# K of four chunks first in token halves, loads in that order, Q's first casts on ScalarE, and a general path without SP

## The chip, the core and the metric

The kernel runs on one core of a Trainium2 chip. The metric is the device time of one execution in microseconds. The core has TensorE (PE; its weight loads are shown apart as PEld), VectorE (DVE), ScalarE (ACT), GpSimd (POOL) and SyncE (SP), which issues all loads and stores of the kernel before. TensorE writes its results into eight banks of PSUM, 512 float32 columns of 128 partitions each; VectorE and ScalarE copy them out.

## What is computed

`x` is 2048 tokens by 512, in bfloat16. Two branches read it, and a gate of one number for each token mixes them:

```python
g = _sigmoid((x * gate_w).sum(-1, keepdims=True))
a = _A_ref(x, A_wq, A_wk, A_wv, A_wo, A_beta)
b = _B_ref(x, B_w_gate, B_w_up, B_w_down)
return g * a + (1 - g) * b
```

`_B_ref` is a gated feed-forward: `(gelu(x @ w_gate) * (x @ w_up)) @ w_down`, with 1792 hidden columns. `_A_ref` is attention with 32 heads of 16 columns in four segments of 512 tokens. Each segment has causal softmax attention of its own, and a memory of the segments before it:

```python
logits = jnp.einsum('bhqd,bhkd->bhqk', qs, ks) * scale + mask
p = _softmax(logits, axis=-1)
a_dot = jnp.einsum('bhqk,bhkd->bhqd', p, vs)
pq = phi(qs)
a_mem = num / den          # pq @ M and pq @ z, M and z summed over earlier segments
o = g * a_mem + (1.0 - g) * a_dot
pk = phi(ks)
M = M + jnp.einsum('bhld,bhle->bhde', pk, vs)
```

with `phi(t) = t + 1` for positive `t` and `exp(t)` otherwise, and at the end `o @ wo`.

## The kernel before

**Layout.** Everything is made segment by segment (`NSEG = 4`, 512 tokens). `xS[s % 3]` holds a segment of `x` with columns on partitions, in four blocks (`FC = 4`). K and Q come in four chunks of 128 columns, eight heads each (`NC8 = 4`): `ktb[:, c, :]` and `QT[:, c, :]`, columns on partitions and 512 tokens along the row. For the logits K is stored once more in `KTm`, which has three places (`NK = 3`), with the columns of even or odd heads set to zero (`eo`): two `tensor_scalar` a chunk, on VectorE for the first three chunks of segment 0 and on GpSimd otherwise.

**PSUM.** The pool `pgen` has four one-bank tiles under the tag `gen`, taken in turn by every matrix product. The pool `plg` has one tile of four banks, `lg`, for the logits.

**Start.** `load_inputs` issues loads on SP: `x` of segment 0 in two halves of 256 tokens, then `wk` in two halves of 256 columns (two chunks each), `wq`, the gate vector, `wv`, `beta`, and `wga` in two parts. `x0` is a borrowed buffer, as `x` comes in with tokens on partitions; `warm_up` runs matmuls on constants meanwhile. `transpose_x0` (L175) turns both halves with 16 TensorE transposes, four copies by VectorE and ScalarE putting them into `xS[0]`; the token order inside a half is two rows a partition (`"(p k) d -> p k d"`). Then, in the order of the program text: `u_k` for chunks 0 to 2 (four matmuls of 512 columns, L368; a cast to `ktb`, L305; two `tensor_scalar` to `KTm`, L378), `u_q` for the four chunks (L282, casts by VectorE), `load_rest` (the other segments' `x` by transposing loads, `wup`, `wdn`, `wo`), the gate vector, V (L397, L413), and the 14 gate chunks of segment 0 (L456) with GELU straight from PSUM on ScalarE (L462).

**The visits.** From there a planner orders the work, while the program is built. 72 visits are fixed; each puts up to four banks of logits into `lg` (`group_qk`, L618), ScalarE takes the exponential (L623), GpSimd zeroes the masked corners (L627), and two visits after a chunk's last piece its product with V follows (`pv`, L643). In between, streams of units (K, Q, V, gate G, up U, down D, output O and others) are filled in by a clock of modelled times: TensorE's and ScalarE's time so far and VectorE's backlog. A unit comes when it is allowed and due; `cast` gives a copy out of PSUM to ScalarE where the model shows room there (`near`), else to VectorE. K's chunk 3 of segment 0 is the first unit of stream K. Stores of the output are issued by `u_out` (L515 makes the tile, L519 issues).

**The two paths.** While the visits run, `u_bound` works out a bound on the logits from the largest values of `x`, `wq` and `wk`. At the end of the program text, VectorE compares it with a limit (L1126), every engine, SP too, loads the flag (L1129) and branches (L1130) past `general()`, a second version of the whole computation with the maximum subtracted. With the inputs here `general()` isn't entered. It issues its loads, transposes and stores on SP.

Of the kernel before, what the change touches and what calls it, by code (L numbers as in the profile page):

```python
# [9 lines left out]
dt = mybir.dt  # L10
AF = mybir.ActivationFunctionType
ALU = mybir.AluOpType

P = 128
# [39 lines left out]
def kernel(  # L54
# [29 lines left out]
    def const(shape, dtype, name):  # L84
        return cpool.tile(shape, dtype, name=name, tag=name)
# [37 lines left out]
    safe = const([1, 1], dt.int32, "safe")  # L123

    def gen(name):
        return pgen.tile([P, 512], F32, name=name, tag="gen")

    def x_seg(s):
        nc.sync.dma_start_transpose(xS[s % NX][:, :, :], x2[s * L:(s + 1) * L, :])
# [4 lines left out]
    def load_inputs():  # L134
        half = L // 2
        for i in range(2):
            nc.sync.dma_start(x0[:, 2 * i:2 * i + 2, :],
                              x2[half * i:half * (i + 1), :].rearrange("(p k) d -> p k d", p=P))
        for i in range(2):
            n = slice(D // 2 * i, D // 2 * (i + 1))  # L140
            cols(wk[:, :, n], A_wk[:, n])
        cols(wq, A_wq)
        nc.sync.dma_start(gw4, gate_w.rearrange("(fc p) -> fc p", p=P))
        cols(wv[:, :, 0:D], A_wv)
        nc.sync.dma_start(beta[:, :], A_beta.rearrange("(o n) -> o n", o=1).to_broadcast((P, H)))
        for n in (slice(0, 4 * P), slice(4 * P, DFF)):
            cols(wga[:, :, n], B_w_gate[:, n])
# [27 lines left out]
    def transpose_x0():  # L175
        for half in range(2):
            for f0 in range(0, FC, 2):
                T = pgen.tile([P, 1024], BF, name="x0T", tag="gen")
                for i in range(4):
                    fc, k = f0 + i // 2, i % 2  # L180
                    nc.tensor.transpose(T[:, i * P:(i + 1) * P],
                                        x0[:, 2 * half + k, fc * P:(fc + 1) * P], ident[:, :])
                dst = xS[0][:, f0:f0 + 2, half * 256:half * 256 + 256].rearrange(
                    "q f (p k) -> q f k p", k=2)
                src = T[:, 0:512].rearrange("q (f k p) -> q f k p", f=2, k=2)
                if f0 == 0:
                    nc.vector.tensor_copy(dst, src)
                else:
                    nc.scalar.copy(dst, src)

    def transpose_gw():
        T = pgen.tile([P, 1024], BF, name="gwT", tag="gen")
# [37 lines left out]
    def u_absmax_x(s, periods):  # L230
# [5 lines left out]
                later(periods[fc] - clock[0], g)  # L236
        return 0.0, 0.0, f

    def u_bound():
        def join():  # L240
            nc.vector.tensor_reduce(out=amax[:, 3:4], in_=amax[:, 3:12], axis=mybir.AxisListType.X,
                                    op=ALU.max)
            nc.vector.tensor_tensor(out=amax[:, 0:1], in0=amax[:, 0:1], in1=amax[:, 3:4],
                                    op=ALU.max)
            passed(0.0, 0.4)

        def narrow():
            nc.vector.tensor_copy(amaxb[:, :], amax[:, 0:3])
            passed(0.0, 0.3)

        def spread():
            room_for_bank()
            T = gen("bT")
            for i in range(3):
                nc.tensor.matmul(T[0:1, i * P:(i + 1) * P], lhsT=amaxb[:, i:i + 1],
                                 rhs=ident[:, :], start=True, stop=True)
            nc.vector.tensor_reduce(out=bound[:, 0:3],
                                    in_=T[0:1, 0:3 * P].rearrange("p (i q) -> p i q", i=3),
                                    axis=mybir.AxisListType.X, op=ALU.max)
            passed(0.15, 0.6)  # L260

        def test():
            nc.vector.tensor_tensor(out=bound[:, 3:5], in0=bound[:, 1:3],
                                    in1=bound[:, 0:1].to_broadcast((1, 2)), op=ALU.mult)
            nc.vector.tensor_tensor(out=bound[:, 5:6], in0=bound[:, 3:4], in1=bound[:, 4:5],
                                    op=ALU.mult)
            passed(0.0, 0.4)

        def f():
            later(1, join)  # L270
            later(3, narrow)
            later(5, spread)
            later(7, test)
        return 0.0, 0.0, f
# [15 lines left out]


    limit = [0.0]
    spared = [0.0]

    def near(end):
# [1 line left out]

    def cast(out, src, scale=1.0):
        end = t_pe[0] + MM512
        if near(end):  # L300
            nc.scalar.activation(out, src, AF.Copy, scale=scale)
            t_act[0] = max(t_act[0], end) + CAST_T
            spared[0] = EVAC
        elif isinstance(scale, float):
            nc.vector.tensor_copy(out, src)  # L305
        else:
            nc.vector.tensor_scalar_mul(out, src, scale)
# [51 lines left out]
    def u_phk(s, c):  # L359
        def f():  # L360
            phi(ktb[:, c:c + 2, :], ktb[:, c:c + 2, :], ("k", s, c), 1)
        return 0.0, 0.0, f

    def u_k(s, c):
        def f():
            T = gen("kT")
            for fc in range(FC):
                nc.tensor.matmul(T[:, :], lhsT=wk[:, fc, c * P:(c + 1) * P],  # L368
                                 rhs=xS[s % NX][:, fc, :],
                                 start=(fc == 0), stop=(fc == FC - 1))  # L370
                if fc < FC - 1:
                    yield MM512
            cast(ktb[:, c, :], T[:, :])
            if general_now[0]:
                return MM512
            for p in range(2):
                eng = nc.vector if s == 0 and c < NK else nc.gpsimd
                eng.tensor_scalar(out=KTm[:, (NC8 * s + c) % NK, :, p, :],  # L378
                                  in0=ktb[:, c, :].rearrange("q (b k) -> q b k", b=NB),
                                  scalar1=eo[:, p:p + 1], scalar2=None, op0=ALU.mult)  # L380
            return MM512
        return 4 * MM512, EVAC, f

    pk_at = {}

    def u_pk(s, c):
        def f():
            assert ("k", s, c - c % 2) in ready
            nc.sync.dma_start_transpose(pk[:, :, c * P:(c + 1) * P], ktb[:, c, :])
            pk_at[s] = clock[0]  # L390
        return 0.0, 0.0, f

# [52 lines left out]
    def u_vs(s):  # L445
        def f():
            v, w = V[s % 2], Vs[s % 2]
            nc.sync.dma_start(w[0:64, :, 0:VE], v[64:128, :, 0:VE])
            nc.sync.dma_start(w[64:128, :, 0:VE], v[0:64, :, VE:2 * VE])
        return 0.0, 0.0, f  # L450

    def u_gate(s, hs, direct):
# [52 lines left out]
    def u_out(s, qt):  # L505
        def f():
            T = gen("aT")
            oT = oTs[s]
            for fc in range(FC):
                nc.tensor.matmul(T[:, :], lhsT=oT[:, fc, qt * P:(qt + 1) * P], rhs=wo[:, fc, :],  # L510
                                 start=(fc == 0), stop=(fc == FC - 1))
                if fc < FC - 1:
                    yield MM512
            osb = tBs[(s, qt)][:, :]
            nc.vector.scalar_tensor_tensor(out=osb, in0=T[:, :],  # L515
                                           scalar=gct[:, s, qt:qt + 1],
                                           in1=osb, op0=ALU.mult, op1=ALU.add)
            q0 = s * L + qt * P
            nc.sync.dma_start(out2[q0:q0 + P, :], osb)  # L519
            return MM512  # L520
        return 4 * MM512, EVAC, f

# [73 lines left out]
    def mem_num(s, c):  # L596
        assert general_now[0] or (count(("Mn", s)) > c // 2 and count(("inv", s)) > c // 2)
        T = gen("mn")
        for qq in range(KT):
# [8 lines left out]
        nc.sync.dma_start_transpose(mT[:, :].rearrange("p (q t) -> p q t", q=KT),  # L608
                                    tm[:, :, :, :].rearrange("p q h d -> p (q h d)"))
        tms[(s, c)] = mT  # L610

    def group_qk(pieces):
# [55 lines left out]
    load_inputs()  # L668
    make_identity(nc, ident[:, :])
    warm_up()  # L670
    transpose_x0()
    setup_consts()


# [91 lines left out]
            for _ in u[2]():  # L766
                pass

    for c in range(NK):
        run(u_k(0, c))  # L770
    for c in range(NC8):
        run(u_q(0, c))
    load_rest()
    transpose_gw()
    for kt in range(KT):
# [289 lines left out]

    def general():
        general_now[0] = True
        nc.gpsimd.memset(Macc[:, :, :, :], 0.0)
        nc.vector.tensor_copy(hm[:, :], bm[:, :, 16])
        for s in range(NSEG):  # L1070
            oT = wk2.tile([P, FC, L], BF, name="oT", tag="oT")
            oTs[s] = oT
            if s % NX == 0:
                x_seg(s)
            for c in range(NC8):
                run(u_k(s, c))
                run(u_q(s, c))
# [40 lines left out]
            if s < NSEG - 1:  # L1118
# [4 lines left out]
                for half in range(2):  # L1123
                    run(u_M(s, half))

    nc.vector.tensor_scalar(out=safe[:, :], in0=bound[:, 5:6],  # L1126
                            scalar1=float(DH ** 0.5 * D * D), scalar2=EXP_LIMIT,
                            op0=ALU.mult, op1=ALU.is_le)
# [31 lines left out]
```

## Time and profile before

| what | value |
|---|---|
| median of 3 runs | 270.8 us (270.6 to 270.86) |
| the profiled execution | 270.57 us |
| its span in the profile | 268.8 us |
| busy: TensorE, VectorE, ScalarE, GpSimd | 262.3, 203.7, 209.0, 156.8 us |
| granted clock of TensorE, mean over the span | 0.996 |
| first K matmul, first Q matmul, first gate matmul | 5.83, 8.50, 15.69 us |
| last output tile made, last store issued | 265.38, 265.41 us |
| DMA | 16.6 MB, mean 62 GB/s over the span |

The span runs from the first instruction that the profiler saw to the last one; the execution's own time is 1.7 us longer. Busy time of TensorE counts a matmul until its modelled end, so that one of 512 columns shows 0.38 us although the next starts 0.216 us after it. In a profile line `L368 PE MATMUL kT<-x,wk` is: line of the kernel, engine, operation, what it writes and reads. `<-` behind an idle time names what ended it.

### The profile page before, as it was taken

What the parts mean: (1) busy time and instruction counts of PE and PEld (TensorE: products, weight loads), DVE (VectorE), ACT (ScalarE), POOL (GpSimd) and SP (SyncE); (2) the same over time, 40 slices, a digit from 0 to 9 for tenths busy, and PEclk for the clock granted to TensorE, in tenths of its full rate; (3) what the DMA queues carried; (4) which work ended last, traced back from release to release, by engine and by line L of the source; (5) the groups of instructions that cost most, each with busy time, mean ns of one, the idle gap of its engine ahead of it and who ended that gap; (6) DMA issues with size and microseconds to landing.
All of it is one profiled execution on the core that took longest, in us unless ns stands there. A gap on an engine that the chain in (4) does not pass through costs nothing.

```text
span 268.8 us, 6576 instructions
## 1 busy us (share of the span) xinstructions
PE 262.3 (98%) x2713; PEld 117.5 (44%) x2713; DVE 203.7 (76%) x390; ACT 209.0 (78%) x163; POOL 156.8 (58%) x298
## 2 busy tenths in 40 slices
PE   7999999999999999999999999999999999999993
PEld 3454434344453444445444444444444544344441
DVE  2999575868777887697986979596898588697374
ACT  3237889999997998889999988889888987567420
POOL 4000168897905979987811998596875089654400
PEclk9999999999999999999999999999999999999998
DMA  6999901200160000301052002110000200001102
GB/s 205 334 211 321 331 18 35 41 4 0 29 136 2 0 22 22 78 4 41 0 68 56 2 21 50 33 34 8 20 24 21 66 2 20 19 3 41 39 22 85
DMA packets 30282, 16.60 MB, mean 62 GB/s; under 512 B 20008, under 2 KB 28968, under 8 KB 30248
## 3 DMA queue, kind: packets, MB, share of 16 engines
q1 hardware_dynamic: 30248, 16.14, 22.9%
q8 instruction: 22, 0.36, 0.6%
q14 instruction: 12, 0.10, 0.1%
HBM read 8.14 MB, written 2.10 MB: 38 GB/s over the span
## 4 chain that ended last, share of the span: by engine, by line
PE 86%; POOL 5%; issue 4%; DMA 2%; ACT 1%; SPq 0%; DVE 0%; ACTq 0%; DVEq 0%; POOLq 0%
PE gT L456 19%; PE uT L477 17%; PE dT L493 14%; PE lg L618 8%; PE od L643 6%; PE aT L510 5%; PE qT L282 5%; PE kT L368 5%; PE vT L397 4%; POOL pT L627 3%; POOL KTm L378 2%; DMA wk<-in_A_wk_dram 2%; PE MT L531 1%; PE mn L600 1%; ACT pT L623 1%
## 5 line engine op out<-in xcount | busy, mean ns | idle before, releaser
L627 POOL TENSOR_SCALAR_AFFINE_SELECT pT<-pT 64x256 bf16<-64x256 bf16 x256 | 113.8, 445 | 94.2 <-ACT pT L623 81.4
L623 ACT ACTIVATE pT<-lg 128x2048 bf16<-128x2048 f32 x72 | 135.1, 1876 | 24.9 <-PE lg L618 21.6
L477 PE MATMUL uT<-x,wup 128*128 128x512 bf16 x224 | 60.4, 380 | 0.0
L456 PE MATMUL gT<-x,wga 128*128 128x512 bf16 x224 | 57.0, 380 | 0.0
L493 PE MATMUL dT<-wdn,G 128*128 128x512 bf16 x224 | 52.9, 380 | 0.0
L483 DVE TENSOR_TENSOR G<-uT,G 128x512 bf16<-128x512 f32 x56 | 38.1, 684 | 6.4 <-PE uT L477 6.2
L378 POOL TENSOR_SCALAR KTm<-ktb,eo 128x512 bf16<-128x512 bf16 x26 | 40.6, 1572 | 1.3
L650 DVE STREAM_TRANSPOSE oq<-od 128x512 f32<-128x512 f32 x32 | 21.0, 695 | 19.5 <-PE od L643 19.5
L493 PEld LDWEIGHTS <-G 128*128 128x128 bf16 x224 | 20.8, 98 | 25.0 <-issue 2.1
L456 PEld LDWEIGHTS <-wga 128*128 128x128 bf16 x224 | 20.5, 98 | 23.9 <-issue 2.2
L477 PEld LDWEIGHTS <-wup 128*128 128x128 bf16 x224 | 19.8, 97 | 24.0 <-issue 5.4
L618 PE MATMUL lg<-QT,KTm 32*128 32x192 bf16 (+7 forms) x512 | 28.5, 287 | 0.0
L305 DVE CAST G<-gT 128x512 bf16<-128x512 f32 x24 | 16.5, 688 | 9.7 <-PE gT L456 9.5
L618 PEld LDWEIGHTS <-KTm 32*128 32x128 bf16 x512 | 8.3, 92 | 28.4 <-issue 28.1
L643 PE MATMUL od<-pT,V 64*32 64x128 bf16 (+7 forms) x512 | 19.4, 284 | 0.2 <-POOL pT L627 0.2
L643 PE MATMUL od<-pT,Vs 64*32 64x128 bf16 (+7 forms) x512 | 19.4, 284 | 0.0
L471 ACT ACTIVATE G<-G 128x3584 bf16<-128x3584 bf16 x6 | 18.8, 3182 | 0.0
L656 DVE SCALAR_TENSOR_TENSOR o<-oq,ogs,rden 128x256 bf16<-128x256 f32 x32 | 17.0, 532 | 1.1
L368 PE MATMUL kT<-x,wk 128*128 128x512 bf16 x64 | 16.8, 380 | 0.9 <-DMA wk<-in_A_wk_dram 0.9
L282 PE MATMUL qT<-x,wq 128*128 128x512 bf16 x64 | 16.6, 379 | 0.0
L515 DVE SCALAR_TENSOR_TENSOR tB<-aT,gct,tB 128x512 bf16<-128x512 f32 x16 | 11.9, 746 | 6.0 <-PE aT L510 5.7
L510 PE MATMUL aT<-wo,oT 128*128 128x512 bf16 x64 | 16.5, 380 | 0.0
(96 smaller groups left out, 274.8 us busy)
## 6 DMA issues: line engine op xcount, KB each, us to landing
out_dram<-tB SPq DMA_DIRECT2D x16, 128.0 KB, 1.7
wup<-in_B_w_up_dram SPq DMA_DIRECT2D x1, 1792.0 KB, 8.4
wdn<-in_B_w_down_dram SPq DMA_DIRECT2D x1, 1792.0 KB
wga<-in_B_w_gate_dram SPq DMA_DIRECT2D x1, 1280.0 KB, 10.2
Vs<-V SPq DMA_DIRECT2D x8, 144.0 KB, 2.6
G<-in_A_x_dram SPq DMA_DIRECT2D x2, 256.0 KB, 2.8
wk<-in_A_wk_dram SPq DMA_DIRECT2D x2, 256.0 KB, 4.2
wq<-in_A_wq_dram SPq DMA_DIRECT2D x1, 512.0 KB, 5.7
```

The lines of the kernel that those rows point to most:

```text
L282: nc.tensor.matmul(T[:, :], lhsT=wq[:, fc, c * P:(c + 1) * P], rhs=xS[s % NX][:, fc, :], start=(fc == 0), stop=(fc == FC - 1))
L368: nc.tensor.matmul(T[:, :], lhsT=wk[:, fc, c * P:(c + 1) * P], rhs=xS[s % NX][:, fc, :], start=(fc == 0), stop=(fc == FC - 1))
L378: eng.tensor_scalar(out=KTm[:, (NC8 * s + c) % NK, :, p, :], in0=ktb[:, c, :].rearrange("q (b k) -> q b k", b=NB), scalar1=eo[:, p:p + 1], ...
L456: nc.tensor.matmul(T[:, :], lhsT=wga[:, fc, hs * P:(hs + 1) * P], rhs=xS[s % NX][:, fc, :], start=(fc == 0), stop=(fc == FC - 1))
L477: nc.tensor.matmul(T[:, :], lhsT=wup[:, fc, hs * P:(hs + 1) * P], rhs=xS[s % NX][:, fc, :], start=(fc == 0), stop=(fc == FC - 1))
L483: nc.vector.tensor_tensor(out=g, in0=T[:, :], in1=g, op=ALU.mult)
L493: nc.tensor.matmul(T[:, :], lhsT=G[s % NG][:, hs, qt * P:(qt + 1) * P], rhs=wdn[:, hs, :], start=(hs == 0), stop=(hs == HS - 1))
L510: nc.tensor.matmul(T[:, :], lhsT=oT[:, fc, qt * P:(qt + 1) * P], rhs=wo[:, fc, :], start=(fc == 0), stop=(fc == FC - 1))
L618: nc.tensor.matmul(lg[:, j, off:off + n], lhsT=KTm[rows, i % NK, b].rearrange("r p k -> r (p k)"), rhs=QT[rows, i % NC8, 64 * b:L], start= ...
L623: nc.scalar.activation(pT[:, :, :], lg[:, :, :], AF.Exp, scale=DH ** -0.5)
L627: nc.gpsimd.affine_select(out=v, in_=v, pattern=[[0, 4], [1, 64]], compare_op=ALU.is_ge, fill=0.0, base=0, channel_multiplier=-1)
L643: nc.tensor.matmul(od[p][32 * j:32 * j + 32, 64 * b:L], lhsT=w[:, 18 * h:18 * h + 32], rhs=t[rows, j, off:off + n], start=(b == 0), stop=( ...
```

## The change

1. `load_inputs` issues `x` half, `wk` half, `x` half, `wk` half, and `wq` in two halves of 256 columns; `x`'s halves are laid out with whole blocks of 128 tokens, `"(k p) d -> p k d"`, so that the copies after the transposes write contiguous tokens.
2. `first_k` replaces `transpose_x0` and the three `u_k`. It takes one four-bank tile of the pool of `lg`, a bank for each chunk. In order: transposes of the first `x` half; the first token half of chunks 0 and 1; transposes of the second half; the first token half of chunks 2 and 3; then the second token half of each chunk, and behind each its copy, on VectorE with the two `KTm` steps for chunks 0 to 2, on ScalarE for chunk 3.
3. Chunk 3's unit in stream K is now `u_km`, only its two `KTm` steps on GpSimd, when a place in `KTm` is free.
4. While the first four `u_q` are issued, `on_act` sends their casts to ScalarE.
5. The flag is computed twice: `is_safe(0)` right after the bound, which GpSimd loads, and `is_safe(1)` at the end for TensorE, VectorE and ScalarE. SP doesn't load the flag. `general()` issues its loads and stores on GpSimd and transposes by TensorE (`turn`).

```diff
     def load_inputs():
...
         for i in range(2):
             nc.sync.dma_start(x0[:, 2 * i:2 * i + 2, :],
-                              x2[half * i:half * (i + 1), :].rearrange("(p k) d -> p k d", p=P))
-        for i in range(2):
+                              x2[half * i:half * (i + 1), :].rearrange("(k p) d -> p k d", p=P))
             n = slice(D // 2 * i, D // 2 * (i + 1))
             cols(wk[:, :, n], A_wk[:, n])
-        cols(wq, A_wq)
+        for n in (slice(0, D // 2), slice(D // 2, D)):
+            cols(wq[:, :, n], A_wq[:, n])
...
+    def is_safe(i):
+        nc.vector.tensor_scalar(out=safe[:, i:i + 1], in0=bound[:, 5:6],
+                                scalar1=float(DH ** 0.5 * D * D), scalar2=EXP_LIMIT,
+                                op0=ALU.mult, op1=ALU.is_le)
...
-            passed(0.0, 0.4)
+            is_safe(0)
+            passed(0.0, 0.5)
...
     def cast(out, src, scale=1.0):
         end = t_pe[0] + MM512
-        if near(end):
+        if on_act[0]:
+            nc.scalar.copy(out, src)
+        elif near(end):
...
+    def first_k():
+        T = plg.tile([P, 4, 512], F32, name="lg", tag="lg")
+
+        def part(c, half):
+            t = slice(256 * half, 256 * half + 256)
+            for fc in range(FC):
+                nc.tensor.matmul(T[:, c, t], lhsT=wk[:, fc, c * P:(c + 1) * P], rhs=xS[0][:, fc, t],
+                                 start=(fc == 0), stop=(fc == FC - 1))
+
+        transpose_x0(0)
+        part(0, 0)
+        part(1, 0)
+        transpose_x0(1)
+        part(2, 0)
+        part(3, 0)
+        for c in range(NC8):
+            part(c, 1)
+            if c < NK:
+                nc.vector.tensor_copy(ktb[:, c, :], T[:, c, :])
+                k_masked(0, c)
+            else:
+                nc.scalar.copy(ktb[:, c, :], T[:, c, :])
...
-            nc.sync.dma_start(out2[q0:q0 + P, :], osb)
+            queue[0].dma_start(out2[q0:q0 + P, :], osb)
...
-    for c in range(NK):
-        run(u_k(0, c))
+    first_k()
     for c in range(NC8):
+        on_act[0] = True
         run(u_q(0, c))
+    on_act[0] = False
...
-        us.append(unit(u_k(s, c), first(i) - 12, ("k", s),
+        us.append(unit((u_km if i < NC8 else u_k)(s, c), first(i) - 12, ("k", s),
...
     def general():
         general_now[0] = True
+        queue[0] = nc.gpsimd
...
-    nc.vector.tensor_scalar(out=safe[:, :], in0=bound[:, 5:6],
-                            scalar1=float(DH ** 0.5 * D * D), scalar2=EXP_LIMIT,
-                            op0=ALU.mult, op1=ALU.is_le)
-    ok = nc.values_load(safe[0:1, 0:1])
+    flag = nc.alloc_registers("safe", engines=[mybir.EngineType.PE, mybir.EngineType.DVE,
+                                               mybir.EngineType.Activation,
+                                               mybir.EngineType.Pool])
+    is_safe(1)
+    for reg in flag:
+        i = 0 if reg.engine == mybir.EngineType.Pool else 1
+        nc.reg_load(reg, safe[0:1, i:i + 1])
+    ok = nc.snap(flag, min_val=0, max_val=1)
     with tc.If(ok == 0, preferred_fallthrough_block=True, label="safe"):
         general()
```

In the built program TensorE's matmuls of the main path are 2713 before and 2729 after.

More of the change, by code (lines that the diff above doesn't have):

```diff
@@ L122 @@
     bound = const([1, 8], F32, "bound")
-    safe = const([1, 1], dt.int32, "safe")
+    safe = const([1, 2], dt.int32, "safe")
     def gen(name):
         return pgen.tile([P, 512], F32, name=name, tag="gen")
+    queue = [nc.sync]
     def x_seg(s):
@@ L173, in warm_up, with transpose_x0 @@
                              start=True, stop=True, tile_position=(64 * r, 32 * j))
[L175 to L189, printed above, removed]
+    def transpose_x0(half):
+        for f0 in range(0, FC, 2):
+            T = pgen.tile([P, 1024], BF, name="x0T", tag="gen")
+            for i in range(4):
+                fc, k = f0 + i // 2, i % 2
+                nc.tensor.transpose(T[:, i * P:(i + 1) * P],
+                                    x0[:, 2 * half + k, fc * P:(fc + 1) * P], ident[:, :])
+            dst = xS[0][:, f0:f0 + 2, half * 256:half * 256 + 256]
+            src = T[:, 0:512].rearrange("q (f t) -> q f t", f=2)
+            if f0 == 0:
+                nc.vector.tensor_copy(dst, src)
+            else:
+                nc.scalar.copy(dst, src)
     def transpose_gw():
@@ L292 @@
     limit = [0.0]
+    on_act = [False]
     spared = [0.0]
@@ L362, in u_phk, with k_masked @@
         return 0.0, 0.0, f
+    def k_masked(s, c):
+        for p in range(2):
+            eng = nc.vector if s == 0 and c < NK else nc.gpsimd
+            eng.tensor_scalar(out=KTm[:, (NC8 * s + c) % NK, :, p, :],
+                              in0=ktb[:, c, :].rearrange("q (b k) -> q b k", b=NB),
+                              scalar1=eo[:, p:p + 1], scalar2=None, op0=ALU.mult)
     def u_k(s, c):
@@ L367, in f @@
             for fc in range(FC):
-                nc.tensor.matmul(T[:, :], lhsT=wk[:, fc, c * P:(c + 1) * P],
-                                 rhs=xS[s % NX][:, fc, :],
+                nc.tensor.matmul(T[:, :], lhsT=wk[:, fc, c * P:(c + 1) * P], rhs=xS[s % NX][:, fc, :],
                                  start=(fc == 0), stop=(fc == FC - 1))
@@ L373, in f, with u_km, turn @@
             cast(ktb[:, c, :], T[:, :])
[L374 to L380, printed above, removed]
+            if not general_now[0]:
+                k_masked(s, c)
             return MM512
         return 4 * MM512, EVAC, f
+    def u_km(s, c):
+        def f():
+            k_masked(s, c)
+        return 0.0, 0.0, f
+    def first_k():
[16 more added lines that the diff above has]
+                k_masked(0, c)
+            else:
+                nc.scalar.copy(ktb[:, c, :], T[:, c, :])
+    def turn(dst, src):
+        T = pgen.tile([P, 1024], BF, name="tT", tag="gen")
+        for i in range(KT):
+            nc.tensor.transpose(T[:, i * P:(i + 1) * P], src[:, i, :], ident[:, :])
+        nc.vector.tensor_copy(dst, T[:, 0:512].rearrange("p (i t) -> p i t", i=KT))
     pk_at = {}
@@ L388, in f @@
             assert ("k", s, c - c % 2) in ready
-            nc.sync.dma_start_transpose(pk[:, :, c * P:(c + 1) * P], ktb[:, c, :])
+            if general_now[0]:
+                turn(pk[:, :, c * P:(c + 1) * P], ktb[:, c, :].rearrange("p (k t) -> p k t", k=KT))
+            else:
+                nc.sync.dma_start_transpose(pk[:, :, c * P:(c + 1) * P], ktb[:, c, :])
             pk_at[s] = clock[0]
@@ L447, in f @@
             v, w = V[s % 2], Vs[s % 2]
-            nc.sync.dma_start(w[0:64, :, 0:VE], v[64:128, :, 0:VE])
-            nc.sync.dma_start(w[64:128, :, 0:VE], v[0:64, :, VE:2 * VE])
+            queue[0].dma_start(w[0:64, :, 0:VE], v[64:128, :, 0:VE])
+            queue[0].dma_start(w[64:128, :, 0:VE], v[0:64, :, VE:2 * VE])
         return 0.0, 0.0, f
@@ L607, in mem_num @@
         mT = wk2.tile([P, L], BF, name="mT", tag="mT")
-        nc.sync.dma_start_transpose(mT[:, :].rearrange("p (q t) -> p q t", q=KT),
-                                    tm[:, :, :, :].rearrange("p q h d -> p (q h d)"))
+        mTv = mT[:, :].rearrange("p (q t) -> p q t", q=KT)
+        if general_now[0]:
+            turn(mTv, tm[:, :, :, :].rearrange("p q h d -> p q (h d)"))
+        else:
+            nc.sync.dma_start_transpose(mTv, tm[:, :, :, :].rearrange("p q h d -> p (q h d)"))
         tms[(s, c)] = mT
@@ L670 @@
     warm_up()
-    transpose_x0()
     setup_consts()
@@ L1073, in general @@
             if s % NX == 0:
-                x_seg(s)
+                rows = G[(s + 1) % NG][:, 0:KT, :]
+                nc.gpsimd.dma_start(rows, x2[s * L:(s + 1) * L, :]
+                                    .rearrange("(k p) d -> p k d", p=P))
+                for fc in range(FC):
+                    turn(xS[s % NX][:, fc, :].rearrange("p (k t) -> p k t", k=KT),
+                         rows[:, :, fc * P:(fc + 1) * P])
             for c in range(NC8):
```

## The prediction

> **What bounds the kernel now.** I read the page's busy shares first, then a table of stretches, then TensorE's waits, then the chain of the first 30 us, and last VectorE's timeline of the start and the program's end. The page's first line of shares:
>
> ```profile
> PE 262.3 (98%) x2713; PEld 117.5 (44%) x2713; DVE 203.7 (76%) x390; ACT 209.0 (78%) x163; POOL 156.8 (58%) x298
> ```
>
> The table of stretches: start and end, length, then busy time and instructions of PE, PEld, DVE, ACT and POOL, granted clock, DMA share, GB/s:
>
> ```profile
> 28.00:120.00 92.00, 92.00 (x998) 40.54 (x995) 70.70 (x134) 82.60 (x62) 66.69 (x120) 1.00 0.20 49
> 120.00:200.00 80.00, 79.98 (x920) 36.30 (x919) 64.31 (x124) 72.34 (x56) 56.45 (x103) 1.00 0.14 30
> 200.00:250.00 50.00, 49.72 (x517) 22.05 (x516) 38.40 (x80) 38.91 (x25) 28.64 (x56) 1.00 0.09 23
> ```
>
> From 28 to 250 us TensorE is hardly ever out of work, while ScalarE and VectorE have 10 to 23% of slack. So whatever delays TensorE's stream before 28 us delays the end by as much, and matmuls taken out of the later stream are saved. TensorE's waits for others (us in total, times, longest), but for one of 1.0 before the warm-up:
>
> ```profile
> PE kT L368 <- DMA wk<-in_A_wk_dram: 0.9, 1, 0.9
> PE od L643 <- POOL pT L627: 0.2, 1, 0.2
> ```
>
> The chain of waits at the start (start, us, what):
>
> ```profile
> 1.71 4.07 DMA wk<-in_A_wk_dram
> 5.78 0.05 issue
> 5.83 2.76 PE kT L368 x12
> 8.59 3.54 PE qT L282 x16
> ```
>
> TensorE waits once, for the first half of `wk`, then runs on without a break: K of three chunks, Q, V. One landing at 5.78 sets when everything starts. VectorE meanwhile (start, duration, instruction):
>
> ```profile
> 6.90 0.69 DVE L305 CAST ktb<-kT 128x512 bf16<-128x512 f32 x1 [1.18 <-PE kT L368]
> 7.63 0.62 DVE L378 TENSOR_SCALAR KTm<-ktb,eo 128x512 bf16<-128x512 bf16 x2
> 8.16 0.69 DVE L305 CAST ktb<-kT 128x512 bf16<-128x512 f32 x1
> 8.88 0.61 DVE L378 TENSOR_SCALAR KTm<-ktb,eo 128x512 bf16<-128x512 bf16 x2
> 9.41 0.68 DVE L305 CAST ktb<-kT 128x512 bf16<-128x512 f32 x1
> ```
>
> It takes 1.26 us a chunk against TensorE's 0.86 (4 matmuls of 0.216), and this costs nothing: each chunk has a bank of its own from a pool of four, so TensorE is at Q's matmuls while VectorE still drains K.
>
> The span is 268.8 us, this execution 270.57, so 1.7 us lie around the span; the median of the runs is 270.8, that is 0.23 above it.
>
> **The start, to the second x half.** The loads go x half, `wk` half, x half, `wk` half. Before, they land at 3.50, 4.17 (x) and 5.78, 6.55 (`wk`), and `wq` at 8.46. After, the first megabyte is the same four pieces, x in rows of 1 KB instead of 2 KB (packets of 46 ns against 84, so about 0.1 us more a half). I expect 3.6, 4.7 to 5.2, 5.3 to 6.0 and 6.7. TensorE's eight transposes of the first half run at 3.85 (0.056 us each); the copies behind them end 1.25 (VectorE) and 1.47 us (ScalarE) after the transposes' start, as in the first half of before (5.02 and 5.24 less 3.77): 5.1 and 5.3. Chunks 0 and 1, first token half: 8 matmuls of 256 columns at half of 0.216, 0.86 us, 5.15 to 6.0. Second transposes to 6.5. Chunks 2 and 3 need the second `wk` half: 6.75 to 7.6. The second half's copies end near 7.5, beside them. So the second token half begins at t0 = 7.6 (7.3 if the contiguous copies are quicker than the 0.72 us of the strided ones and `wk` lands early; 8.3 if pieces land 0.7 us late, as `wk`'s first half did when 1.61 us passed between it and the x half before it).
>
> **The second token half is the large term.** All four chunks now lie in one four-bank tile `T` of the pool `lg`. In the built program's list of instructions and waits, the first matmul of chunk 1's second half waits for VectorE's copy of chunk 0, chunk 2's for the copy of chunk 1, chunk 3's for that of chunk 2: the tile is guarded as a whole, though each chunk has its own bank. Behind the waiting matmul stand, in TensorE's order, the other chunks, then Q, V and everything else. One round: three matmuls until the last one starts 0.32, its completion 0.27 (0.379 for 512 columns at a pitch of 0.216 leaves 0.16 of latency, plus 0.107), handover 0.04 (6.87 to 6.90), copy 0.69, handover 0.05 (5.78 to 5.83): 1.37 us. VectorE's own round of 1.26 fits inside it. Without the wait it would be 0.43. Three rounds and a last 0.43: Q's matmuls begin at 7.6 + 3 x 1.37 + 0.43 = 12.15 instead of 8.50: **+3.65 us**. A round lies between 1.26 (VectorE alone) and 1.45.
>
> The Trainium skill, "PSUM — Partial Sum Buffer" (Terms, PSUM bank), keeps engines apart per bank and quadrant alone; by it these waits aren't needed and the start would come out as in the first rival. The trace agrees on the rule (chunk 1's matmuls at 6.70 run while VectorE casts chunk 0 at 6.90), but the wait is in the program.
>
> **Chunk 3 of K** leaves the later stream, where TensorE has no gap to hide it: 4 x 0.216 = **-0.86 us**. If TensorE then merely idles there, 0. `k_masked` stays on GpSimd for it (2 x 1.57 us, idle 42% of the span), due at the same visit.
>
> **Q's casts on ScalarE.** Four of about 0.69 us (L301's length) and chunk 3's copy go there, 3.4 us. ScalarE takes chunk 3 at 12.4, Q from 13.2 to about 16.5, then `eb` 0.23 and a table load of 1.28, done at 18.0; its first GELU is wanted at about 20.3. V's first bank must be free at 15.7 and is at 14.8; the last V bank is wanted at 18.0, free at 16.5. So nothing; without that cover up to 0.7. VectorE loses 2.48 us of casts, where it limits nothing.
>
> **The loads behind.** One more issue on SP's queue (0.5 us) and `wq` in 512-byte pieces move `wv` from 9.84 to about 10.4 and the first `wga` part from 12.5 to 13.2; they are wanted at 15.8 and 19.3. The transposing loads of x behind them wait for a VectorE memset that now comes at about 12.3 (13.1 before). Nothing.
>
> **The program's end.** The last rows are
>
> ```profile
> 264.63 0.75 DVE L515 SCALAR_TENSOR_TENSOR tB<-aT,gct,tB 128x512 bf16<-128x512 f32 x1
> 265.29 0.13 DVE L1126 TENSOR_SCALAR safe<-bound 1x1 int32<-1x1 f32 x1
> 265.41 0.33 SPq L519 DMA_DIRECT2D out_dram<-tB  x1
> ```
>
> The last store lands 1.67 us after its issue, at 267.08. SP loads the flag and branches until 266.46, and from 266.93 goes through eight semaphore waits of L1130 and eight of L1155, 0.06 to 0.09 us each, to 268.09; a closing barrier follows. After, SP has no flag and no L1130; it has four waits for GpSimd's DMA counts, which pass at once, and eight for its own. The last of 65 loads and stores counts on the first of these eight, so seven remain after its landing: 7 x 0.063 and two drains of 0.07, 267.68: **-0.4 us** (0 to -0.6). GpSimd's early flag, load and branch (0.49 + 0.05 us) and its setting of those counts come after its last select at 253.1, with 12 us of cover; with the late flag SP's four waits would stand behind it, 0.5 us at most. The general path is not entered; its longer lists cost nothing that a row shows.
>
> **The order of the work between.** The planner's visits are shuffled from about visit 5 to the last fifth (the last 64 groups of TensorE are alike). The old order loses 0.3 us or more in one go at three places only, 1.1 us in all, so I take 0, between -0.6 and +0.6.
>
> **Sum.** 3.65 - 0.86 - 0.4 = +2.4 us: 272.95 for a profiled execution like this one, 273.2 on the median.
>
> **Rivals.** (1) *The waits cost nothing*, because VectorE is done in time or the order holds without them: Q begins at 7.6 + 4 x 0.43 = 9.33, +0.83; less 0.86 and 0.4 that is -0.4; ScalarE's Q casts then queue behind VectorE's three rounds (chunk 3's copy waits for chunk 2's) and V's first bank comes up to 0.4 late: 270.4 to 270.8, not slower, below 270.2 only with t0 at 7.3. It decides if a round takes under 0.6 us. Against it: the cast alone takes 0.69. Chance 0.08.
> (2) *The clock falls.* Three idle stretches of 0.94 us between 8 and 12 us: if TensorE then ran at the 0.43 us a matmul of the warm-up rows (2.31 us for 5) for 2.2 us or until Q's end, 1.1 to 3.5 us more: about 275.5. Against it: 1.08 us of idling at 4.75 was followed by matmuls at 0.216, granted clock 1.00. Chance 0.04. The Trainium skill, "TensorE: Matmul & The Clock Gate" (A second HAM failure mode), tells of such falls from short idling between groups of matmuls; the trace's one gap didn't show it.
> (3) *Chunk 3's time isn't got back*, because ScalarE's exponentials pace the visits: 273.2 + 0.86 = 274.1. For it: ScalarE is 90% busy from 28 to 200. Against: TensorE is 100% busy there. Chance 0.10.
>
> **How the numbers follow.** The forecast's case has 0.72, these three 0.22, and 0.06 is for what I don't see (a planner order that wins or loses over 0.6 us). Its own bounds, taken together as squares: down 0.3 (t0), 0.33 (rounds), 0.2 (end), 0.6 (order): 0.8; up 0.7, 0.24, 0.4, 0.6: 1.0. With rival 3 inside, the range is 272.2 to 274.4. A measurement of this kernel can tell about 0.2% (0.54 us) from no change: faster by more 0.04 (half of rival 1, and a lucky order), within 0.06, slower 0.90.
>
> **What would show it.** In the profile after: TensorE idle 0.9 us before three of the K matmuls, each ended by VectorE's copy of `ktb`; VectorE's copies about 1.37 apart; Q's first matmul near 12.15; the first gate matmul near 19.3 (15.69); from the last store's issue to the span's end 3.0 us instead of 3.4. Wrong if K's matmuls of the second half follow each other without waits, if Q's matmuls take 0.43 us, or if the stretch from the first gate matmul to the last output matmul isn't 0.9 us shorter.

## The result, and the profile after

The changed kernel takes 275.04 us (median of six executions, 274.40 to 276.25) against 270.77 us for the kernel before in the same job (six executions, 270.51 to 270.90): a ratio of 1.0153, 95% interval 1.0127 to 1.018. It is slower, as forecast, but by 4.3 us where the sum had 2.4, and 275.04 lies 0.64 us above the range. The profiled execution took 274.40, the shortest of the six. That matters below: a second profile shows where a usual one loses more.

The page's first line of shares:

```profile
PE 263.6 (97%) x2729; PEld 119.4 (44%) x2729; DVE 201.3 (74%) x387; ACT 210.5 (77%) x167; POOL 156.6 (57%) x298
```

TensorE is as dominant as before. The same table of stretches (start and end, length, busy time and instructions of PE, PEld, DVE, ACT and POOL, granted clock, DMA share, GB/s):

```profile
28.00:120.00 92.00, 92.00 (x980) 40.33 (x979) 69.04 (x128) 81.78 (x65) 62.54 (x111) 1.00 0.20 46
120.00:200.00 80.00, 79.49 (x924) 36.52 (x923) 64.75 (x123) 71.34 (x54) 56.99 (x104) 1.00 0.13 30
200.00:250.00 50.00, 49.21 (x516) 21.86 (x514) 39.81 (x84) 38.61 (x26) 28.93 (x57) 1.00 0.09 23
```

The second and third stretch have lost 0.5 us of TensorE's time each: 79.98 and 49.72 became 79.49 and 49.21. Small as that looks, it is where the largest miss of the forecast lies. TensorE's waits (us in total, times, longest) name both losses; the wait for the engine's own start and one of 0.3 are left out:

```profile
PE lg L405 <- DVE ktb L417: 2.3, 3, 0.8
PE uT L524 <- ACT V L310: 1.0, 2, 0.5
...
PE od L693 <- POOL pT L677: 0.2, 1, 0.2
PE lg L405 <- DMA wk<-in_A_wk_dram: 0.2, 1, 0.2
```

The first line is the wait that the prediction described. The second was not in it. A wait counts here from the modelled end of the last matmul, so the stream loses more than the line says: 0.95 us three times in the first, 0.68 us twice in the second, counted from where the next matmul could have started.

The chain of waits at the start (start, us, what):

```profile
2.34 4.54 DMA wk<-in_A_wk_dram
6.88 0.05 issue
6.93 1.50 PE lg L405 x12
8.43 0.02 issue
8.45 0.70 DVE ktb L417
9.15 0.04 issue
9.20 0.61 PE lg L405 x4
9.81 0.02 issue
9.83 0.70 DVE ktb L417
```

Matmuls and copies take turns: four matmuls, VectorE's copy, four matmuls. The copies start at 8.45, 9.83 and 11.21, so a round is 1.38 us (forecast 1.37), and Q's first matmul is at 12.39 (forecast 12.15, before 8.50).

What the two waits of the second kind are, in the timeline of ScalarE and then of TensorE around 131 us (start, duration, instruction, idle time before):

```profile
129.78 1.88 ACT L673 ACTIVATE pT<-lg 128x2048 bf16<-128x2048 f32 x1 [0.25 <-PE lg L668]
131.56 0.54 ACT L310 ACTIVATE V<-vT 128x448 bf16<-128x448 f32 x1
```

```profile
130.77 0.36 PE L444 MATMUL vT<-wv,x 128*128 128x448 bf16 x1
130.97 0.67 PE L578 MATMUL MT<-V,pk 128*128 128x136 bf16 x8
132.15 0.38 PE L524 MATMUL uT<-x,wup 128*128 128x512 bf16 x1 [0.51 <-ACT V L310]
```

V's matmuls end at 131.1. The planner has given their cast to ScalarE, which is in an exponential from 129.78, so the cast starts only at 131.56 and ends at 132.10. Of the four banks of `pgen`, the next one `uT` needs is the one this cast empties, and TensorE stands still from the end of MT's matmuls to 132.15. The same happens at 200.0 to 200.74. In the order of before, no `uT` matmul waits for a cast of V.

The program's end:

```profile
268.87 0.75 DVE L562 SCALAR_TENSOR_TENSOR tB<-aT,gct,tB 128x512 bf16<-128x512 f32 x1
269.54 0.13 DVE L240 TENSOR_SCALAR safe<-bound 1x1 int32<-1x1 f32 x1
```

The last store is issued at 269.65 and the span ends 3.02 us later, instead of 3.43.

So the span splits in three: the start, the work from the first gate matmul to the last store, and the end. The experiments are in the same table.

| us | first K, first Q matmul | first gate matmul | last store issued | gate to last store | last store to span end | median |
|---|---|---|---|---|---|---|
| before | 5.83, 8.50 | 15.69 | 265.41 | 249.72 | 3.43 | 270.77 to 270.84 |
| changed | 4.89, 12.39 | 19.57 | 269.65 | 250.09 | 3.02 | 275.04 |
| changed, second profile (f6) | 4.89, 12.96 | 20.13 | 270.25 | 250.12 | 3.02 | 274.99 |
| e1: copies last | 4.89, 10.07 | 17.25 | 267.33 | 250.08 | 3.02 | 272.21 |
| e2: order of before | 4.89, 13.03 | 20.20 | 269.70 | 249.51 | 3.02 | 274.45 |
| e3: e1 and e2 | 4.89, 10.14 | 17.31 | 267.18 | 249.87 | 3.02 | 271.72 |
| e4: flag alone | 6.07, 8.67 | 15.85 | 265.56 | 249.71 | 2.60 | 269.99 |
| f1: e1, two casts out | 4.89, 10.08 | 17.25 | 266.51 | 249.26 | 3.02 | 271.31 |
| f4: e4, `wq` in halves | 5.94, 8.54 | 15.72 | 265.43 | 249.71 | 3.02 | 270.40 |

### The profile page after: what moved, and what is told of

It reads as the page before. It is cut to its first block, busy times and chain, and to the rows that moved or that the text cites. A ratio compares the mean times of both kernels' runs of the same rounds, so it can differ in the third digit from the quotient of the medians.

```text
span 272.7 us, 6617 instructions
## 1 busy us (share of the span) xinstructions
PE 263.6 (97%) x2729; PEld 119.4 (44%) x2729; DVE 201.3 (74%) x387; ACT 210.5 (77%) x167; POOL 156.6 (57%) x298
## 4 chain that ended last, share of the span: by engine, by line
PE 84%; POOL 5%; issue 4%; ACT 2%; DMA 2%; DVE 1%; SPq 1%; ACTq 0%; DVEq 0%; POOLq 0%
PE gT L503 18%; PE uT L524 17%; PE dT L540 14%; PE lg L668 8%; PE od L693 5%; PE aT L557 5%; PE qT L288 5%; PE vT L444 4%; PE kT L384 3%; POOL pT L677 3%; POOL KTm L376 2%; ACT pT L673 2%; DMA wk<-in_A_wk_dram 2%; PE lg L405 1%; PE MT L578 1%
## 5 line engine op out<-in xcount | busy, mean ns | idle before, releaser
L314 DVE CAST G<-gT 128x512 bf16<-128x512 f32 x27 | 18.5, 685 | 5.9 <-PE gT L503 5.7
L693 PEld LDWEIGHTS <-V 64*32 64x32 bf16 x512 | 13.1, 92 | 5.9 <-issue 3.5
```

The source lines that it names most:

```text
L693: nc.tensor.matmul(od[p][32 * j:32 * j + 32, 64 * b:L], lhsT=w[:, 18 * h:18 * h + 32], rhs=t[rows, j, off:off + n], start=(b == 0), stop=( ...
```

## The experiments

The theory after the first profile: (A) the start loses what the shared tile's waits cost, (B) the gain of chunk 3 is eaten by the two V casts that the reshuffled order puts behind an exponential, (C) the end gains what SP no longer does. The rival to B is that TensorE was held up by ScalarE in any order, so that chunk 3's time could never be got back.

**e1, the copies after all matmuls (A).**

```diff
         for c in range(NC8):
             part(c, 1)
+        for c in (3, 0, 1, 2):
             if c < NK:
```

> The changed kernel, but first_k issues the second token halves of all four chunks before any copy, then the copies (ScalarE's chunk 3 first, then VectorE's three). TensorE's matmuls then wait for no copy. Theory A (the three waits on the shared tile cost about 2.85 us): Q's first matmul moves from 12.39 to about 9.6 us and the median from 275.0 to about 272.2. Rival B (the time is lost behind the start): median stays within 0.5 us of 275.0. If the idle stretches at the start also cause the spread of the runs (274.4 to 276.25) by lowering TensorE's clock in some executions, the spread shrinks to some 0.4 us and the mean clock is 1.00 in all runs.

Measured: 272.21 us (five executions, 271.89 to 272.26), ratio 1.0045 (1.0032 to 1.0058). TensorE's timeline:

```profile
4.89 1.68 PE L405 MATMUL lg<-x,wk 128*128 128x256 bf16 x8
6.56 0.62 PE L182 MATMUL x0T<-ident,G 128*128 128x128 bf16 x8
7.44 2.79 PE L405 MATMUL lg<-x,wk 128*128 128x256 bf16 x24 [0.26 <-DMA wk<-in_A_wk_dram]
```

The 24 later matmuls follow each other with no wait, and Q starts at 10.07. The expected 9.6 was taken from the changed kernel's first profile; here the second half of `wk` lands at 7.40 instead of 6.88. The median of 272.2 was met, as the usual execution of the changed kernel loses that time too (f6 below). The same copies are made on the same engines, three of them at the same 0.69 us, and 2.8 us of the 4.3 are gone. A is shown: the waits, not the amount of work, cost this. The executions lie within 0.37 us of each other, as the text expected if the gaps also caused the spread of the changed kernel's; its other sign, a mean clock of 1.00 in all of them, did not come (two have 0.997; in the profiled one of these the only half clock recorded comes at the end, from 268.91 us on).

**e2, the order of before (B); e3, both.** The planner is told that `u_km` still takes four matmuls and a cast, and the bound as long as before; nothing of chunk 3's matmuls or cast is issued. All work behind the start then comes in the order of before, with a hole at chunk 3's old place. (Theory C of the two texts that follow is B here.)

```diff
             is_safe(0)
-            passed(0.0, 0.5)
+            passed(0.0, 0.4)
...
     def u_km(s, c):
         def f():
+            for fc in range(FC - 1):
+                yield MM512
+            end = t_pe[0] + MM512
+            if near(end):
+                t_act[0] = max(t_act[0], end) + CAST_T
+                spared[0] = EVAC
             k_masked(s, c)
-        return 0.0, 0.0, f
+            return MM512
+        return 4 * MM512, EVAC, f
```

> The changed kernel, but the planner is told that chunk 3 of K still takes four matmuls and a cast at its old place (nothing is computed there), so that all later work stands in exactly the order of before. Theory C (the shuffled order costs TensorE two stalls of 0.68 us behind V's casts on ScalarE): the stalls are gone, the stretch from the first gate matmul to the last output tile is 0.86 us shorter than before's, and the median is about 273.7. Rival D (order is noise, the rest comes from elsewhere): 275.0.

> Both edits of the two runs before. If A and C add up: 275.0 - 2.85 - 1.3, about 270.9. If the old order gives TensorE nothing once its start is early (it waits for ScalarE's exponentials instead): about 272.

Measured: e2 274.45 us (four executions, 273.92 to 274.48), ratio 1.0126 (1.0111 to 1.0141); e3 271.72 (seven, 271.43 to 272.05), ratio 1.003 (1.0019 to 1.0041). Gate to last store is 249.51 and 249.87 in place of 250.09: the two V waits are gone, but most of the 0.86 isn't back. e3's 0.36 over e2 is one more wait for GpSimd, at 230.6 us. e2's timeline of ScalarE and of TensorE shows why:

```profile
44.88 1.88 ACT L680 ACTIVATE pT<-lg 128x2048 bf16<-128x2048 f32 x1 [0.17 <-PE lg L675]
```

```profile
45.63 0.59 PE L510 MATMUL gT<-x,wga 128*128 128x512 bf16 x2
46.81 0.40 PE L675 MATMUL lg<-QT,KTm 32*128 32x512 bf16 x4 [0.58 <-ACT pT L680]
```

The next logits need the banks of `lg`, and the exponential holds them until 46.76. Chunk 3's four matmuls had filled that time, as the chain of the kernel before shows at the same place:

```profile
40.31 0.97 PE kT L368 x4
41.28 0.86 PE qT L282 x4
42.15 0.43 PE gT L456 x2
```

Without them TensorE stands 0.74 us. So in the old order the rival holds: there ScalarE's exponential sets the pace at that place.

**f1, e1 without the two casts (B, directly).** V's chunk 2 in segments 2 and 3 isn't cast, so those rows keep what an earlier segment left; the time is what is read here.

```diff
         elif near(end):
-            nc.scalar.activation(out, src, AF.Copy, scale=scale)
+            if not skip:                     # u_v: skip=(s, kt) in ((2, 2), (3, 2))
+                nc.scalar.activation(out, src, AF.Copy, scale=scale)
```

> The changed kernel with its copies in an order of their own (as e1_copies_last), and two of V's casts left out: chunk 2 of segments 2 and 3, the two that ScalarE made behind an exponential while TensorE stood at uT (0.68 us each, at 129.1 and 197.7 us of e1_copies_last). The rows of V that they would write keep what an earlier segment left there. Everything else stays in its place. Theory (the two stalls are what ate the gain of the removed K chunk): no gap between MT and uT at those two places, first gate matmul to last store 248.7 instead of 250.08, median 272.21 - 1.36 = 270.85. Rival (TensorE would meet another wait at once, the casts only showed it): 0.5 us or less comes back, 271.7 or more, and gate to last store stays above 249.5.

Measured: 271.31 us (twelve executions, 270.64 to 271.56), ratio 1.0 (0.9979 to 1.0022); gate to last store 249.26. That lies between the two expectations: 0.82 of the 1.36 us came back. Neither place shows a wait any more, but a new one is there 5 us behind the first. VectorE, then TensorE:

```profile
134.44 0.68 DVE L533 TENSOR_TENSOR G<-uT,G 128x512 bf16<-128x512 f32 x1
```

```profile
135.17 0.59 PE L527 MATMUL uT<-x,wup 128*128 128x512 bf16 x2 [0.44 <-DVE G L533]
```

VectorE empties an older `uT` at 134.44 to 135.12, as in e1 (134.41), where TensorE came 0.7 us later and found the bank free. Of the first place's 0.68 us, 0.60 is paid again to VectorE; the second place's 0.68 is a true gain. Without this wait gate to last store would be 248.66 by these rows, 1.06 under before; no run shows that. So B is right about what held TensorE, and the rival about half of what a removed wait is worth.

**e4, the flag and SP's part alone on the kernel before (C); f4, the same with `wq` in two loads.** e4 is the kernel before with part 5 of the change. f4 adds

```diff
-        cols(wq, A_wq)
+        for n in (slice(0, D // 2), slice(D // 2, D)):
+            cols(wq[:, :, n], A_wq[:, n])
```

> The kernel before with only the last part of the change: SP out of the general path, early flag for GpSimd, general path with GpSimd's loads and TensorE's transposes; same order of work as before. Theory E: from the last store's issue to the span's end 3.0 instead of 3.4 us, median 270.4. Rival F (the closing barrier ends with another engine, or GpSimd's part of the path costs as much): 270.8.

> The kernel before with the SP-free general path and early flag alone (as e4_flag_only), and wq's load in two halves: 65 loads and stores by SP in place of 64. Theory (the program's end reads one semaphore after another, and the last store's place among the eight decides how many are read after it): last store to span end 3.0 instead of 2.60, median 269.99 + 0.42 = 270.4, the rest unchanged. Rival (the end is shorter for another reason in e4_flag_only, the load order or the start): 2.6 again, 270.0.

Measured: e4 269.99 us (twelve executions, 269.74 to 272.15) against 270.83 in its job, ratio 0.9979 (0.9958 to 1.0001), last store to span end 2.60. f4 270.40 (twelve, 270.11 to 270.67), ratio 0.9971 (0.9951 to 0.9992), end 3.02. The trace of SP's closing reads explains the 0.42. In e4 the last of 64 loads and stores is counted on the last of eight semaphores; by its landing at 267.23 the other seven have been read (266.18 to 267.01), and the eighth at 267.25 is the last. In f4 the last of 65 is counted on the first; SP waits there until the landing at 267.09 and then reads seven more, 0.06 us each, to 267.53. C is shown. The 3.0 and 270.4 expected for e4 were missed: they held the reads that follow in a kernel with 65 loads and stores, and e4 has 64. The interval of e4's ratio just reaches 1, f4's doesn't. The end is two terms: -0.83 for SP out of the last path, +0.42 for one load more.

**f6, the changed kernel again.**

> The changed kernel once more, unaltered, for a second profile, because its first profiled execution (274.40) was the shortest of six with a median of 275.04. Theory (in a usual execution the second half of x lands later, as in e1, e2 and e3, at 6.5 to 6.6 where the first profile had 6.10): begin of the second token half at about 8.3, Q's first matmul at 12.8 to 13.1, span 273.1 to 273.4, and gate to last store 250.0 to 250.2 as before. Rival (the start is the same and the rest varies): Q at 12.4, and gate to last store 250.5 or more.

Measured: the profiled execution 275.13, span 273.28, Q at 12.96, gate to last store 250.12; all as expected. The chain's two lines that differ:

```profile
2.34 5.11 DMA wk<-in_A_wk_dram
...
7.50 1.50 PE lg L405 x12
```

`wk`'s second half lands at 7.45 instead of 6.88, and `x`'s second half at 6.56 instead of 6.10. All of the 0.6 us between the two spans is there. e1, e2, e3 and f1 had 6.46 to 6.64 too, so the first profile is the exception, and the later start is the usual one.

**f2, g1, g2, g3: why the loads land late.** Before, the third load landed at 5.78. Is it the pieces of 1 KB, or the order? f2 and g2 are e1 with `x` in pieces of 2 KB, `"(p k) d -> p k d"`, and the strided copies of before; g3 is e1 with both `x` halves ahead of both `wk` halves; g1 is e1 again.

```diff
# g3
             nc.sync.dma_start(x0[:, 2 * i:2 * i + 2, :], ...)
+        for i in range(2):
             n = slice(D // 2 * i, D // 2 * (i + 1))
```

> The changed kernel with its copies in an order of their own (as e1_copies_last), and x loaded in rows of two tokens (2 KB pieces) as in the kernel before, so that the copies of the transposes are strided again; the order of the loads stays the new one. Theory (the pieces of 1 KB make x's second half land late, 6.5 us in e1, e2 and e3 against 5.8 to 6.0 for the third load of the old order): x's second half lands at 5.8 to 6.0, Q's first matmul at 9.7 to 9.9 (0.5 earlier landing, 0.3 back in the strided copy), median 272.0. Rival (the size of the pieces does nothing; the third load is late for another reason): it lands at 6.3 to 6.6 again, Q at 10.1 to 10.4, median 272.2 to 272.5.

> e1_copies_last once more, unaltered, on the same chip as the two that follow, since f2 (median 272.57) and e1 (272.21) were timed in different jobs. Both theories: x's second half lands at 6.4 to 6.6, Q's first matmul at 10.0 to 10.3, median 272.2 to 272.4.

> f2_2kb_rows once more (e1 with x in pieces of 2 KB, the copies strided). Theory (1 KB pieces delay x's second half): it lands at 5.9 to 6.1 again, Q at 9.7 to 9.9, and the median is 0.2 to 0.4 under g1's. Rival (one profile's chance): it lands at 6.3 to 6.6, and the median is g1's or up to 0.3 above it, because of the strided copies.

> e1 (x in pieces of 1 KB) with the loads in the order of the kernel before: both halves of x, then both halves of wk. Theory (what the start pays beside the waits is the order: x's second half comes third instead of second, and 16 first-half and second-half groups can't run until it is there): x's second half lands at 4.2 to 4.4, wk's halves at 5.8 to 6.1 and 6.6 to 6.9, K's matmuls run from 5.9 without a break for 3.5 us, Q's first matmul at 9.4 to 9.6, median 271.6 to 271.8. Rival (the order costs nothing; the start is bound by copies or by TensorE): Q at 10.0 to 10.3, median that of g1.

| us | x's second half lands | wk's halves land | first Q matmul | median |
|---|---|---|---|---|
| g1: 1 KB, new order | 6.67 | 4.61, 7.51 | 10.18 | 272.31 (five) |
| f2: 2 KB, new order | 5.99 | 4.43, 7.03 | 9.77 | 272.57 (ten) |
| g2: 2 KB, new order | 5.75 | 4.54, 6.68 | 10.63 | 272.33 (five) |
| g3: 1 KB, order of before | 4.33 | 6.99, 7.79 | 12.65 | 274.09 (four) |

On the landings the first theory holds: with 2 KB the third load is there at 5.75 to 5.99, with 1 KB at 6.46 to 6.67 in six profiles (e1, e2, e3, f1, f6, g1) and at 6.10 in one, the changed kernel's first. Behind two 1 KB halves of `x` (g3) `wk` lands at 6.99; behind two 2 KB halves it came at 5.78 (before), 6.02 (e4) and 5.90 (f4). On the time it fails: g2 is no faster than g1 (272.33, 272.31), and f2's median of 272.57 isn't either. The strided copies take 0.73 us where the contiguous ones take 0.42, and in g2 the eight matmuls before them were slow as well:

```profile
5.20 1.86 PE L406 MATMUL lg<-x,wk 128*128 128x256 bf16 x8 [0.39 <-DVE x L188]
```

They follow each other at 0.207 us, start to start, against 0.109 in f2, and the second transposes, landed or not, stand behind them on TensorE. g2's profiled execution is the longest of its five, f2's the shortest of its ten. So an earlier landing is only sometimes worth anything.

g3 missed both expected times. TensorE waits for `wk` until 7.04 and then runs at half speed until about 11. Stretches of TensorE (start and end, length, busy time and instructions, granted clock, DMA share, GB/s):

```profile
5.00:7.00 2.00, 0.00 (x0) 1.00 1.03 298
7.00:9.00 2.00, 1.96 (x12) 0.55 1.04 282
9.00:11.00 2.00, 2.00 (x16) 0.59 0.67 116
11.00:13.00 2.00, 2.00 (x19) 1.00 1.05 388
```

After 2.65 us of idling the granted clock is 0.55 and 0.59; the trace's clock records have one stretch at half, from 7.21 to 10.62. In this profile K's 32 matmuls and eight transposes take 5.6 us (7.04 to 12.65), where 32 at 0.109 and eight at 0.056 would be 3.9, and the expectation had 3.5 without the transposes. `wk`'s first half, at 6.99 instead of 5.8 to 6.1, is the rest of the miss. That the clock costs the 1.8 us by which the medians differ is not shown: the profiled execution is the longest of g3's four (274.67, mean clock 0.994), and the other three, with a mean clock of 1.00, still took 274.05 to 274.10. Their matmuls may have been slow ahead of the first clock record, where the mean counts full speed (see the last section); no profile of them exists, and no run tried g3 with TensorE kept busy.

## Why the prediction was wrong, by its own steps

- **The second token half: right.** Three rounds of 1.38 us (1.37), each for VectorE's copy on the tile guarded as a whole; e1 took the waits away and got 2.8 us back. (The sum's 12.15 is 12.14 by its own terms; nothing hangs on it.) Rival 1 would have needed a round under 0.6.
- **The begin of the second half, t0: undersized.** Forecast 7.6 (7.3 to 8.3). Taking three rounds and a last 0.43 from Q's first matmul, it is 7.82 in the first profile and 8.39 in the second. The term that was too small is the landing of `wk`'s second half, which TensorE waits for: 6.7 forecast, 6.88 and 7.45 measured. Ahead of it in the queue, the second half of `x` landed at 6.10 and 6.56, where the forecast had 5.3 to 6.0 and "about 0.1 us more a half" for rows of 1 KB; with rows of 2 KB it landed at 5.75 and 5.99. The quicker contiguous copies (0.42 instead of 0.72) gave nothing back here: they end at 7.39 and 7.85, before TensorE has gone through the chunks that waited for `wk`. The start came to +3.89 and +4.46 us, not +3.65.
- **Chunk 3 and the order of work between: the step that failed.** The prediction took -0.86 for the chunk and 0, between -0.6 and +0.6, for the planner's shuffling. Measured together: 250.09 - 249.72 = +0.37, in the second profile +0.40, so 1.2 us were missing. It is the sign that the prediction itself named: this stretch isn't 0.9 us shorter. The shuffled order put two casts of V on ScalarE behind exponentials, 0.68 us each, and f1, without the two, got 0.82 us back. The prediction followed the built program's instructions only through the start and summed the rest by size; which casts ScalarE gets behind an exponential, and that the next `uT` takes their bank, stands in the same lists.
- **Rival 3 (chunk 3's time isn't got back)** had the right size for this stretch and half the mechanism. In the order of before, an exponential takes the place of the chunk's matmuls (e2, 0.74 us); in the changed kernel it acts through a cast queued behind it. Its time of 274.1 lacked the later t0.
- **The end: right in sum,** -0.41 against -0.4.
- **Q's casts on ScalarE, the loads behind: right at nothing.** From Q's first matmul to the first gate matmul it is 7.18 us (12.39 to 19.57) against 7.19 before.
- **Rival 2 (the clock falls): not in the two profiled executions.** There the granted clock was 1.00 after three gaps of 0.95 us, and Q's matmuls ran at 0.216. But two of the ten executions of the changed kernel, 276.25 and 276.03 us, have a mean clock of 0.994; the other eight have 0.999 or 1.00 and took 274.40 to 275.17. One stretch of 3.41 us at half clock gives such a mean in g3's profile, so the clock probably fell in these two as well; no profile shows where or after what. The Trainium skill, "TensorE: Matmul & The Clock Gate" (A second HAM failure mode), tells of falls from short idle gaps between groups of matmuls; in the two profiles these three gaps did not show it. One gap of 2.65 us, in g3, was followed by half the clock.

The sum as it was, with the start taken to the first gate matmul: +3.88 + 0.37 - 0.41 = +3.84 for the first profile (spans 272.7 and 268.8), and +4.44 + 0.40 - 0.41 = +4.43 for the second (273.3). The medians differ by 4.27, which lies between the two.

Of the parts that were run apart, only part 5 pays: e4 at 269.99 us is the fastest of all versions run, 0.84 under before by the medians, and f4's `wq` in halves takes 0.41 of it back.

## What to carry to other kernels

When a planner reorders work, the cost can lie not in the step that was taken out but in which copies now queue behind a long instruction: list the casts that moved, and for each the next matmul that needs its bank. A wait that is removed is worth its length only if the next engine in line is ahead: f1 got 0.82 of 1.36 us back. And chunks that share one tile are one resource: issue all their matmuls before the first copy out of it, or take a tile for each (not run here).

## What was not expected of the hardware

- **Semaphores at the end have an order.** Which semaphore the last store counts on decided 0.42 us: one more load, 64 to 65, moved it from the last of eight to the first, with seven reads of 0.06 us behind it. The prediction had counted these seven; what they cost is what e4 and f4 showed.
- **Pieces of 1 KB against 2 KB** moved the landing of the third load of 256 KB by 0.5 to 0.9 us (6.46 to 6.67 in six profiles of seven, against 5.75 and 5.99; the seventh had 6.10), though the first one lands at 3.44 to 3.78 us with either.
- **A granted clock of 1.00 at the start can mean that nothing was recorded yet.** The first K matmuls follow each other at 0.21 us in some executions and at 0.109 in others, in stretches whose granted clock reads 1.00. In the traces the change from one pace to the other falls on the first clock record, to about 0.1 us: 6.08 us in e1, 6.76 in e2, 6.97 in g2, and 4.25 in the changed kernel's first profile, where all K matmuls are fast. Ahead of that record there is none, and the views show 1.00. Why it comes at a different time in each execution stays open.
- **Contiguous copies out of PSUM are quicker on VectorE above all:** 0.42 us in place of 0.72 for the same 512 columns, on ScalarE 0.59 in place of 0.73.
